# Four buffers in place of two for softmax numerators ahead of their DMA transposes

## The chip, the cores and the metric

One core of a Trainium2 chip. The metric is the device time of one execution in microseconds (us). Each run also records the mean clock granted to TensorE (1.0 is full). Engines in the profile: PE is TensorE, PEld its weight loads, DVE VectorE, ACT ScalarE, POOL GpSimd, SP SyncE; SPq is SyncE's queue of DMA issues. PSUM is, in this kernel, the memory that holds TensorE's scores and products.

## The reference, cut to what matters

```python
scores = (q @ k.T) / sqrt(64)                  # 8 batches x 8 heads, 576 x 576 each
scores = where(scores >= max(scores) - 0.02, scores, -1e9)
attn = exp(scores - max(scores)); attn /= attn.sum(-1)
x = (attn @ v) laid out as (8, 576, 512)
# then, per batch: h = relu(x @ w_in); u, v = halves of h; v normalized over features,
# mixed over positions by w_spatial plus a bias; out = (u * mixed v) @ w_out
```

The output is float32, 8 x 576 x 512.

## The kernel before

Two heads are a pair; there are 32 pairs. A pair's 512 first rows are four chunks of 128 (c = 0 to 3); the last 64 rows of two pairs share a chunk c = 4, worked in the odd pair. One chunk is one *step*, 144 in all; the steps of an odd pair come in the order 4, 0, 1, 2, 3. In a step TensorE makes the scores `s`, VectorE the maxima, ScalarE the exponentials. The numerators go to a buffer `p`, two chunks each, and one DMA transpose moves a full buffer to `pT`, which TensorE takes as weights for the product with v.

```python
p_ring = [const.tile([P, 2, 1152], BF16, name=f"p{i}") for i in range(2)]   # chunks 0,1 | 2,3
ptp = ctx.enter_context(tc.tile_pool(name="ptp", bufs=5))                    # pT
...
def mask():                                    # for the chunk of the step before
    i, c, e = unmasked.pop()
    ...
    pt = p_ring[c // 2]
    if not on_act(c):                          # chunks 0, 1, 3: VectorE writes p  (L541)
        nc.vector.scalar_tensor_tensor(out=pt[:, c % 2, :], in0=ef, scalar=ctau, in1=ef, ...)
    if c % 2:                                  # buffer full: transpose, from SyncE (L545)
        dst = pts[i, c // 2] = ptp.tile([P, 2, 9, P], BF16, name="pT")
        nc.sync.dma_start_transpose(out=..., in_=pt...)
...
def step(i, c, fs):
    s = scores(i, c)                           # TensorE (L519, L524)
    ...                                        # maxima on VectorE (L560)
    if on_act(c):                              # chunks 2 and 4
        for h in range(2): nc.scalar.activation(out=e[:, h, :], ..., func=ACT.Prelu, ...)  # L577
        nc.scalar.activation(out=pr_ring[i // 2 % 2] if c == 4 else p_ring[c // 2][:, c % 2],
                             in_=e..., func=ACT.Exp)                                       # L579
    else:
        for h in range(2): nc.scalar.activation(out=e[:, h, :], ..., func=ACT.Exp, ...)    # L583
    ...
    if unmasked: mask()
```

So chunk 2 is written by ScalarE in its own step, the others by VectorE one step late. The transpose of chunks 2 and 3 of an odd pair is issued in step 0 of the next pair, and ScalarE writes that buffer again in step 2.

## Time and profile before

| | before |
|---|---|
| timed runs, first call | 500.39, 500.67, 501.63, 503.14 us |
| profiled execution | 506.3 us (span 504.5), clock 0.973, state slow |
| TensorE, VectorE, ScalarE busy | 91%, 82%, 76% of the span |
| ScalarE idle before L579, for a transpose | 13.4 us in 6 places |
| VectorE idle before L541, for a transpose | 1.6 us in 1 place |

Busy shares say which engine is fullest. The idle time *before* an instruction, with what ended it, says which wait exists. Neither says alone what a wait costs. An engine *stands* while it is idle like this, and one such place is a *stop*. The lines are in the prediction below.

### The profile page before, as it was taken

The numbers are of one execution on the slowest core, as the hardware profiler recorded it, in microseconds if no ns is written. First come the engines' busy times: TensorE is split into PE (matmuls) and PEld (weight loads), VectorE is DVE, ScalarE is ACT, GpSimd is POOL, SyncE is SP. The second block draws the span as 40 slices with busy tenths as digits, with TensorE's granted clock in tenths as the row PEclk, the third lists the DMA queues.
The fourth block names the chain that finished last, engine by engine and source line by source line (L and its number), as shares of the span: only waits on it lengthen the run. The fifth ranks groups of instructions, "written<-read, shape, count | busy, mean of one in ns | idle before, by whom it ended". The sixth has DMA issues, their size and how long they took to land.

```text
span 504.5 us, 9916 instructions
## 1 busy us (share of the span) xinstructions
PE 459.3 (91%) x3672; PEld 244.8 (49%) x3672; DVE 412.4 (82%) x559; ACT 381.1 (76%) x665; POOL 224.5 (44%) x406
## 2 busy tenths in 40 slices
PE   7786977889988999979999999999999999997996
PEld 4342534445554545535455555545454545544543
DVE  2896696988989888868898888898889988897473
ACT  2784576798977888868887889787987889795251
POOL 3543312579535743246425753276425753251021
PEclk9997797999999999989999999999999999998999
DMA  7399789797999998987979998898987898667313
GB/s 229 64 222 244 176 174 180 197 212 162 203 193 205 169 210 170 186 158 160 224 178 194 181 201 191 192 196 170 220 201 176 179 214 181 136 119 116 116 63 126
DMA packets 231041, 89.38 MB, mean 177 GB/s; under 512 B 200593, under 2 KB 225169, under 8 KB 230993
## 3 DMA queue, kind: packets, MB, share of 16 engines
q1 hardware_dynamic: 230416, 87.93, 82.4%
q8 instruction: 29, 0.48, 0.4%
q0 software_dynamic: 160, 0.52, 0.3%
q10 hardware_dynamic: 416, 0.30, 0.2%
q14 instruction: 20, 0.16, 0.1%
HBM read 33.31 MB, written 9.44 MB: 85 GB/s over the span
## 4 chain that ended last, share of the span: by engine, by line
PE 51%; ACT 20%; DVE 12%; DMA 11%; issue 5%; POOL 0%; ACTq 0%; POOLq 0%; DVEq 0%
PE s L524 15%; DMA pT<-p 11%; ACT e L583 6%; DVE negm L560 6%; PE f L235 5%; PE s L519 5%; PE f L493 4%; DVE p L541 4%; PE f L268 3%; PE f L464 3%; ACT e L577 3%; PE f L434 3%; ACT vrel L402 2%; PE f L392 2%; ACT sq L416 2%
## 5 line engine op out<-in xcount | busy, mean ns | idle before, releaser
L560 DVE TENSOR_REDUCE negm<-s 128x2 f32<-128x1152 f32 x144 | 194.7, 1353 | 44.6 <-PE s L524 44.3
L524 PE MATMUL s<-qkT 64*128 64x512 f32 (+1 forms) x640 | 165.7, 651 | 0.0
L541 DVE SCALAR_TENSOR_TENSOR p<-e,ctau 128x1152 bf16<-128x1152 f32 x96 | 138.1, 1438 | 4.1 <-ACT e L583 2.2
L583 ACT ACTIVATE e<-s,negm 128x576 f32<-128x576 f32 x192 | 131.5, 739 | 6.3 <-DVE negm L560 6.2
L519 PE MATMUL s<-kd,qkT 128*128 128x128 f32 (+1 forms) x320 | 65.2, 308 | 18.0 <-ACT e L583 11.0
L577 ACT ACTIVATE e<-s,negm 128x576 f32<-128x576 f32 x96 | 65.7, 738 | 20.1 <-DVE negm L564 12.6
L258 POOL COPY kd<-qkT 64x64 f32<-64x64 f32 x64 | 27.8, 435 | 109.3 <-ACT qkT L253 107.3
L519 PEld LDWEIGHTS s<-kd,qkT 128*128 128x128 f32 (+1 forms) x320 | 45.8, 184 | 38.6 <-ACT e L583 21.6
L524 PEld LDWEIGHTS s<-qkT 64*128 64x128 f32 (+1 forms) x640 | 42.6, 177 | 18.6 <-issue 3.6
L268 PEld LDWEIGHTS <-pT 128*128 128x128 bf16 x1024 | 43.2, 99 | 10.8 <-issue 7.4
L579 ACT ACTIVATE p<-e 128x1152 bf16<-128x1152 f32 x32 | 37.2, 1164 | 14.3 <-DMA pT<-p 13.4
L410 POOL TENSOR_SCALAR nmean<-sm 128x1 f32<-128x1 f32 (+1 forms) x35 | 14.7, 420 | 73.3 <-ACT vrel L402 73.3
L268 PE MATMUL f<-v,pT 128*128 128x65 bf16 x992 | 46.3, 197 | 0.0
L138 POOL COPY qn<-ql 128x640 f32<-128x640 f32 x32 | 35.5, 1108 | 11.8 <-issue 6.5
L263 PE MATMUL f<-v,pT 128*128 128x130 bf16 x124 | 27.6, 223 | 11.0 <-ACT vrel L402 5.8
L464 PE MATMUL f<-wsT,vn 128*128 128x512 bf16 x120 | 30.9, 389 | 3.7 <-ACT qkT L253 3.7
L240 ACT ACTIVATE qkT<-f 128x512 f32<-128x512 f32 x32 | 18.9, 590 | 19.5 <-PE f L235 19.5
L242 ACT COPY qkT<-f 128x512 f32<-128x512 f32 x32 | 18.7, 586 | 17.3 <-PE f L235 17.2
L148 POOL CAST v<-vl 128x640 bf16<-128x640 f32 x32 | 30.1, 942 | 0.1
L422 POOL TENSOR_SCALAR vn<-vrel,rs,nm 128x512 bf16<-128x512 f32 (+1 forms) x34 | 27.4, 805 | 3.7
L392 PE MATMUL f<-w_in,xT 128*128 128x512 bf16 x112 | 28.9, 380 | 0.0
L434 PE MATMUL f<-xT,w_in 128*128 128x512 bf16 x108 | 27.9, 380 | 0.9 <-DVE xn L277 0.9
(155 smaller groups left out, 639.9 us busy)
## 6 DMA issues: line engine op xcount, KB each, us to landing
vl<-in_v_dram SPq DMA_DIRECT2D x16, 512.0 KB, 4.6
ql<-in_q_dram SPq DMA_DIRECT2D x15, 512.0 KB, 4.7
kl<-in_k_dram SPq DMA_DIRECT2D x15, 512.0 KB, 4.5
out_dram<-o SPq DMA_DIRECT2D x20, 256.0 KB, 3.1
uT<-in_moe_w_in_dram SPq DMA_DIRECT2D x3, 512.0 KB, 5.7
uT<-in_moe_w_spatial_dram SPq DMA_DIRECT2D x2, 576.0 KB, 5.8
vl<-in_v_dram SPq DMA_DIRECT2D x16, 64.0 KB, 4.3
pT<-p SPq DMA_TRANSPOSE x64, 5.0
```

The lines of the kernel that those rows point to most:

```text
L138: nc.gpsimd.tensor_copy(out=t, in_=ld_ring[i // 2 % 2][w][:, 2 * (i % 2):2 * (i % 2) + 2].rearrange("p h c d -> p c h d"))
L268: nc.tensor.matmul(out=t[:, at + 65 * h:at + 65 * h + 65], lhsT=pt[:, 5 * h + j, :], rhs=vt[:, 6 * h + j, :], start=False, stop=(h == 1 an ...
L392: nc.tensor.matmul(out=t, lhsT=xts[b][:, f, c * P:(c + 1) * P], rhs=w_in[:, f, 512:1024], start=(f == 0), stop=(f == 3))
L434: nc.tensor.matmul(out=t, lhsT=w_in[:, m, f * P:(f + 1) * P], rhs=xts[b][:, m, 0:512], start=(m == 0), stop=(m == 3))
L464: nc.tensor.matmul(out=t, lhsT=vn[:, c, f * P:(f + 1) * P], rhs=wsT[:, c, 0:512], start=(c == 0), stop=(c == 4))
L519: nc.tensor.matmul(out=view(s[rows], 512, [[448, 2], [1, 64]]), lhsT=qks[n][:, 0, m], rhs=kd_ring[n % 2], start=True, stop=True)
L524: nc.tensor.matmul(out=s[rows, 1024 * h:1024 * h + 512], lhsT=qks[n][hs, 0, m], rhs=qks[n][hs, 1, 0:512], start=True, stop=True)
L541: nc.vector.scalar_tensor_tensor(out=pt[:, c % 2, :], in0=ef, scalar=ctau, in1=ef, op0=ALU.is_ge, op1=ALU.mult)
L560: nc.vector.tensor_reduce(out=nm, in_=s, axis=AX.X, op=ALU.max, negate=True)
L577: nc.scalar.activation(out=e[:, h, :], in_=s[:, h, :], func=ACT.Prelu, bias=nm[:, h:h + 1], scale=by, alpha=1e30)
L579: nc.scalar.activation(out=pr_ring[i // 2 % 2] if c == 4 else p_ring[c // 2][:, c % 2], in_=e.rearrange("p h s -> p (h s)"), func=ACT.Exp)
L583: nc.scalar.activation(out=e[:, h, :], in_=s[:, h, :], func=ACT.Exp, bias=nm[:, h:h + 1])
```

## The change

The intent is that a write of numerators never waits for the transpose that still reads the buffer: each buffer comes again after two pairs (about 28 us) in place of one. Nothing else changes; the order of instructions on every engine is the same.

```diff
-    p_ring = [... for i in range(2)]
+    p_ring = [... for i in range(4)]
-        pt = p_ring[c // 2]
+        pt = p_ring[2 * (i % 2) + c // 2]
-            nc.scalar.activation(out=pr_ring[i // 2 % 2] if c == 4 else p_ring[c // 2][:, c % 2],
+            nc.scalar.activation(out=pr_ring[i // 2 % 2] if c == 4 else p_ring[2 * (i % 2) + c // 2][:, c % 2],
```

More of the change, by code (lines that the diff above doesn't have):

```diff
@@ L66 @@
     mhalf = const.tile([P, 1], F32, name="mhalf")
-    p_ring = [const.tile([P, 2, 1152], BF16, name=f"p{i}") for i in range(2)]
+    p_ring = [const.tile([P, 2, 1152], BF16, name=f"p{i}") for i in range(4)]
     pr_ring = [const.tile([P, 1152], BF16, name=f"pr{i}") for i in range(2)]
```

## The prediction

> **What bounds the kernel now.** I read the page first: its engine table, then the groups of instructions, then the chain that ended last.
>
> ```profile
> PE 459.3 (91%) x3672; PEld 244.8 (49%) x3672; DVE 412.4 (82%) x559; ACT 381.1 (76%) x665; POOL 224.5 (44%) x406
> ...
> PE 51%; ACT 20%; DVE 12%; DMA 11%; issue 5%; POOL 0%; ACTq 0%; POOLq 0%; DVEq 0%
> PE s L524 15%; DMA pT<-p 11%; ACT e L583 6%; DVE negm L560 6%; PE f L235 5%; PE s L519 5%; PE f L493 4%; DVE p L541 4%; PE f L268 3%; PE f L464 3%; ACT e L577 3%; PE f L434 3%; ACT vrel L402 2%; PE f L392 2%; ACT sq L416 2%
> ...
> pT<-p SPq DMA_TRANSPOSE x64, 5.0
> ```
>
> TensorE is the fullest engine, but the chain gives 11% of the span, 55 us, to the transposes of the numerators, the transfers whose source buffers the change doubles. That share is not what the change can win: the chain names a whole transfer as soon as it is the last releaser, even if the engine behind it stood for a moment. The view of the waits by releaser counts only standing time:
>
> ```profile
> ACT p L579 <- DMA pT<-p: 13.4, 6, 4.3
> ...
> PEld L263 <- DMA pT<-p: 9.6, 5, 3.3
> ```
>
> and the view of the tile p adds one VectorE wait of 1.6 us (L541). So at most 15.0 us of standing, in seven places, is the write-after-read wait on p. Six come before ScalarE's L579 (numerators of chunk 2, even pairs): by the timeline at 44.3 to 48.6 us (4.29), 75.1 to 78.2 (3.10), 158.8 to 160.7 (1.90), 216.6 to 219.8 (3.11), and 0.44 and 0.51 near 276 and 332 us. The other 26 writes by L579 wait for nothing. The even pairs suffer because chunk 2 of pair i+1 comes two steps after the transpose of chunks 2 and 3 of an odd pair i is issued, against three steps the other way round.
>
> Next question: what does TensorE do in those places? This is the timeline around the third.
>
> ```profile
> 159.76 1.09 PE L524 MATMUL s<-qkT 64*64 64x512 f32 x8
> ...
> 160.66 1.16 ACT L579 ACTIVATE p<-e 128x1152 bf16<-128x1152 f32 x1 [1.90 <-DMA pT<-p]
> 160.77 0.10 PEld L263 LDWEIGHTS <-pT 128*128 128x128 bf16 x1 [0.81 <-DMA pT<-p]
> ...
> 161.73 0.58 ACT L402 ACTIVATE vrel<-f 128x512 f32<-128x512 f32 x1
> ...
> 162.46 0.22 PE L263 MATMUL f<-v,pT 128*128 128x130 bf16 x1 [1.61 <-ACT vrel L402]
> ```
>
> TensorE has run ahead by two score blocks and then wants the product with pT of the previous odd pair: the result of the very transfer that ScalarE waits for. It landed at 160.58. From then TensorE is held only because its PSUM bank is to be freed by vrel (L402), which stands behind L579 in ScalarE's order. A part of each stop therefore stays after the change, as a read-after-write wait of TensorE, and only the part after the landing can go.
>
> **What the Trainium skill says.** (1) "TensorE: Matmul & The Clock Gate", Architectural detail under Part 1: "ACT/DVE are strict FIFO", and TensorE reorders weight loads only. The trace agrees: vrel at 161.73, whose product had ended by 158.84, waited behind L579. (2) Same page, Part 1, on the clock gate: the clock falls to half after about one idle window of 3413 ns, the window runs free, and a busy window restores it. The trace agrees in kind: the windows view shows granted clock 0.50 from about 44 to 57.6 us and 78 to 84.5 us, and 0.51 at 222 to 225 us, each after such a stop, and four score matmuls take 2.08 us there in place of 1.13. (3) "DMA: Bandwidth & Descriptors", Anatomy of one DMA: a semaphore wait happens on the issuing sequencer before dispatch. The trace agrees: the transpose issued at 40.44 us stands behind four loads of 0.5 to 0.6 us each on SyncE and lands 8.0 us after its issue. The buffer count of p changes nothing in that queue.
>
> ```profile
> 42.00:45.00 3.00, 0.78 (x12) 0.35 (x8) 2.97 (x4) 1.37 (x2) 0.17 (x1) 0.84 1.17 208
> 45.00:48.00 3.00, 1.93 (x10) 0.25 (x8) 1.90 (x4) 0.00 (x0) 1.72 (x3) 0.50 1.08 244
> ...
> 57.00:60.00 3.00, 3.00 (x28) 1.36 (x26) 2.04 (x5) 1.33 (x4) 1.43 (x4) 0.89 1.02 249
> ```
>
> (Columns: window, length, then busy time of TensorE, weight loads, VectorE, ScalarE and GpSimd, granted clock, DMA share, GB/s. ScalarE is at 0.00 in the second line: that is the stop.)
>
> **The change part by part.** *Added and removed instructions*: none. The order of instructions on all five engines is the same in both kernels; only buffer names and a few waits differ. Three waits of the writers of p go because they are first uses, one each appears on the writers of pr and of two outputs, and four on xr; all of these name transfers of buffers last used about a pair of pairs earlier (some 28 us), so I count them as zero. *Memory*: two more buffers of 2x1152 bf16, 4.6 KB a partition each; it builds. *Moved*: a write of p now waits for a transpose two pairs back, some 28 us, against landings of 4.6 to 8.4 us. All seven waits should go: 15.0 us of standing to zero.
>
> *What that is worth on the path*, by stop, as TensorE's idle time after the landing:
> - 48 us: after pT lands the product runs 48.5 to 49.8; the next scores wait 1.23 us for e (L583), which stood behind L579. Gain 1.23.
> - 78 us: the same picture, 1.23.
> - 160 us: TensorE is free at 160.85, starts at 162.46. Gain 1.61.
> - 219 us: landing 219.69, start 221.54 behind vrel. Gain 1.83.
> - 276 and 332 us: 0.16 and 0.22.
> Sum 6.3 us. VectorE's 1.6 us at 39.9 counts nothing extra: TensorE would only reach the 48.5 us landing earlier and stand longer.
>
> *Clock*: at 219 us the idle falls from 3.27 to about 1.4 us, like the 1.61 us at 160 us that lost no clock. The work after 221.54 ran at half clock (L464 x5 2.32 us in place of 1.24, products 1.1 in place of 0.6); without that, about 1.6 us less. At 48 and 78 us the long idle stays, but TensorE then works without the second gap, and may get its clock back one window earlier; one window at half speed is 1.7 us of lost work each, and I give that four chances in ten: 1.4. Ceiling by this trace 6.3 + 1.6 + 1.4 = 9.3 us.
>
> *Cut*: this profiled run took 506.3 us, 4.7 over the median of the timed runs, so some of these stops, most likely that at 219 us with its clock loss (3.4 us), are smaller or absent there. Without it: 9.3 - 3.4 = 5.9. Not all will be kept, as VectorE is nearly full in the first 100 us (2.9 to 3.0 of 3 us in most windows outside the stops) and the DMA engines are 83 to 95% busy; I keep eight tenths: 4.8 us. Predicted 501.63 - 4.8 = 496.8 us, 1% less.
>
> **The rivals.**
> *A: the wait only changes hands.* The products need the same transposes two steps later, and DMA or SyncE sets the pace; TensorE's waits for pT grow by what ScalarE's shrink. For it: DMA at 0.95 in 104 to 160 us, the shared landing in the timeline, transposes held in SyncE's order. Against it: in four of six stops TensorE demonstrably stands 1.2 to 1.8 us after the landing, and later stretches without stops have TensorE at 54.5 of 56 us. Then 500 to 501.6 us.
> *B: the loops tighten more than the sum says.* ScalarE comes earlier to the numerators of chunk 3's partner, so the next transpose is issued earlier, later stops shrink too, and the two cold stretches (about 13.6 and 6.5 us at half clock) vanish altogether, worth up to 10 us. For it: the cold stretch at 44 us begins just when TensorE stands 2.23 us behind ScalarE and VectorE's delayed work. Against it: pT lands at 48.5 whatever p does, so TensorE is idle some 4 us there anyway. Then 489 to 492 us.
> *C: slower.* Earlier transposes collide with loads. Against it: the traffic and its order are the same, and SyncE issues strictly in order. At most 1 or 2 us.
>
> **Range and chances.** A and the sum bound the likely region: 492.5 to 500.8 us. A gain over 2% means under 491.6 us, that is B nearly whole: 0.07. Slower by 2% (over 511.7) has no mechanism here: 0.01. Within 2%: 0.92.
>
> **What would show it.** Right: no wait of L579 or L541 for pT<-p; the transposes' share of the chain gone from ScalarE and coming back, smaller, through L263; TensorE's waits for pT the same or larger in sum (now 12.7 us); vrel no longer releasing L263 for over 1 us; steady batches still 55.5 to 56 us. Wrong, towards A: the waits at L263 grow by 10 us or more and the span stays. Wrong, towards B: granted clock near 1.0 through 44 to 85 us. The prediction fails too if the unprofiled runs have stops in other places than this one trace.

## The result, and the profile after

| | before | after |
|---|---|---|
| median of the first call | 501.15 us (4 runs) | 488.84 us (4 runs: 488.69, 488.74, 488.93, 496.58) |
| ratio of the fast runs | | 0.9747, 95% interval 0.9711 to 0.9784 |

Ratios here are the mean time of one kernel's fast runs over that of the other's of the same rounds, so not quite the ratio of the medians quoted. A run counts as slow when it is over 1.5% above its kernel's fastest.

From the page of the kernel after: the engines, the chain that ended last, and the group of L579, whose last column (idle before it) names no transpose any more.

```profile
PE 451.2 (93%) x3672; PEld 240.6 (49%) x3672; DVE 413.4 (85%) x559; ACT 382.0 (78%) x665; POOL 228.7 (47%) x406
...
PE 46%; DVE 23%; ACT 18%; issue 6%; DMA 4%; SPq 2%; POOL 0%; DVEq 0%; ACTq 0%
...
L579 ACT ACTIVATE p<-e 128x1152 bf16<-128x1152 f32 x32 | 37.2, 1164 | 1.0
```

The view of the waits of the kernel after has neither L579 nor L541 waiting for pT<-p. What is left of the waits for transposes is TensorE's:

```profile
PEld L263 <- DMA pT<-p: 5.6, 4, 2.3
...
PE f L263 <- DMA pT<-p: 2.2, 2, 1.4
```

Before, these were 9.6 and 3.1 us. So TensorE's waits for the same transposes did not grow in exchange; in this profile they shrank. Over all profiles they neither shrank nor grew clearly: 12.7, 7.2 and 6.4 us before, 7.8, 8.2, 10.7 and 8.0 us after (one stop can count under both PEld and PE). This is the timeline at the place that the prediction showed (chunk 2 of pair 10, then the product of pair 9):

```profile
149.81 1.17 ACT L579 ACTIVATE p<-e 128x1152 bf16<-128x1152 f32 x1
...
150.78 1.09 PE L524 MATMUL s<-qkT 64*64 64x512 f32 x8
...
150.88 0.58 ACT L402 ACTIVATE vrel<-f 128x512 f32<-128x512 f32 x1
...
151.79 0.10 PEld L263 LDWEIGHTS <-pT 128*128 128x128 bf16 x1 [0.81 <-DMA pT<-p]
151.80 0.23 PE L263 MATMUL f<-v,pT 128*128 128x130 bf16 x1
```

L579 waits for nothing, vrel (L402) follows it 1.07 us later, the bank is free, and the product starts as soon as TensorE has ended its scores. TensorE wants pT 2.0 us after ScalarE wanted the buffer (151.80 against 149.81); in those 2.0 us the transpose lands.

A place-by-place comparison: I took the start of the chunk 2 write of each pair from the timelines (L579; L540 in the kernel that moves it). "To pair 5" is the first six pairs with the start of the kernel; "5 to 31" the other 26. The last column adds up the idle time before that write for a transpose, within 5 to 31.

| profile | to pair 5, us | 5 to 31, us | 13 to 31, us | ScalarE standing in 5 to 31, us |
|---|---|---|---|---|
| before, first (slow) | 93.3 | 365.7 | 255.9 | 5.96 |
| before (ctrl_before, slow) | 88.4 | 366.7 | 257.2 | 6.74 |
| before (before_second, slow) | 91.3 | 361.7 | 252.6 | 3.27 |
| two buffers with fillers (warm_before, fast) | 90.4 | 362.9 | 254.1 | 3.94 |
| after, first (fast) | 83.8 | 359.3 | 250.8 | 0 |
| after_again, after_third, after_fourth (fast) | 86.5, 85.3, 85.7 | 359.6, 358.9, 358.6 | 250.8, 250.8, 250.8 | 0 |

From pair 13 on the kernel after takes 250.8 us in every profile. The kernel before takes 1.8 to 6.4 us more, and over 5 to 31 its excess over the mean of the four (359.1) is 6.6, 7.6 and 2.6 us for 5.96, 6.74 and 3.27 us of standing. The three profiles of the kernel before fell on runs that count as slow (499.9 to 506.3 us), so the difference must also show in a fast one. It does: warm_before, described below, took 500.3 us and counts as fast, its additions all come before chunk 2 of pair 5, and its 5 to 31 is 3.8 us over for 3.94 us of standing. The first six pairs wander in both.

### The profile page after: what moved, and what is told of

It reads as the page before. It is cut to its first block, busy times and chain, and to the rows that moved or that the text cites. A ratio compares the mean times of both kernels' runs of the same rounds, so it can differ in the third digit from the quotient of the medians.

```text
span 486.9 us, 9920 instructions
## 1 busy us (share of the span) xinstructions
PE 451.2 (93%) x3672; PEld 240.6 (49%) x3672; DVE 413.4 (85%) x559; ACT 382.0 (78%) x665; POOL 228.7 (47%) x406
## 4 chain that ended last, share of the span: by engine, by line
PE 46%; DVE 23%; ACT 18%; issue 6%; DMA 4%; SPq 2%; POOL 0%; DVEq 0%; ACTq 0%
PE s L524 13%; DVE negm L560 11%; DVE p L541 8%; PE f L235 5%; PE f L493 4%; ACT e L583 4%; PE s L519 4%; ACT e L577 4%; PE f L268 3%; DMA pT<-p 3%; PE f L434 3%; PE f L464 3%; ACT sq L416 2%; ACT vrel L402 2%; ACT qkT L242 1%
## 5 line engine op out<-in xcount | busy, mean ns | idle before, releaser
L524 PE MATMUL s<-qkT 64*128 64x512 f32 (+1 forms) x640 | 163.8, 642 | 0.0
L541 DVE SCALAR_TENSOR_TENSOR p<-e,ctau 128x1152 bf16<-128x1152 f32 x96 | 140.2, 1461 | 1.5 <-ACT e L583 1.2
L268 PEld LDWEIGHTS <-pT 128*128 128x128 bf16 x1024 | 41.9, 98 | 7.2 <-issue 3.9
L268 PE MATMUL f<-v,pT 128*128 128x65 bf16 x992 | 44.9, 194 | 0.0
L579 ACT ACTIVATE p<-e 128x1152 bf16<-128x1152 f32 x32 | 37.2, 1164 | 1.0
L464 PE MATMUL f<-wsT,vn 128*128 128x512 bf16 x120 | 29.8, 378 | 3.7 <-ACT qkT L253 3.7
L277 DVE TENSOR_TENSOR xn<-f,r 128x256 bf16<-128x256 f32 x62 | 26.3, 425 | 2.1
L422 POOL TENSOR_SCALAR vn<-vrel,rs,nm 128x512 bf16<-128x512 f32 (+1 forms) x34 | 26.3, 772 | 3.7
```

The source lines that it names most:

```text
L268: nc.tensor.matmul(out=t[:, at + 65 * h:at + 65 * h + 65], lhsT=pt[:, 5 * h + j, :], rhs=vt[:, 6 * h + j, :], start=False, stop=(h == 1 an ...
L464: nc.tensor.matmul(out=t, lhsT=vn[:, c, f * P:(f + 1) * P], rhs=wsT[:, c, 0:512], start=(c == 0), stop=(c == 4))
L524: nc.tensor.matmul(out=s[rows, 1024 * h:1024 * h + 512], lhsT=qks[n][hs, 0, m], rhs=qks[n][hs, 1, 0:512], start=True, stop=True)
```

## The experiments

My theory after the result: the gain is ScalarE's standing before L579, as everything behind it in ScalarE's order stands too, plus what the loss of TensorE's clock after such a stop adds. Rivals: VectorE's one wait starts the first stop; the clock alone is the gain; the first result was luck.

| run | what differs from the kernel before | mean us (runs) | before in the same call | ratio of fast runs, 95% |
|---|---|---|---|---|
| ctrl_before | nothing | 499.5 (22) | 499.2 (59) | 0.997 (0.994 to 1.001) |
| p1_only | chunks 2, 3 doubled | 492.0 (6) | 499.2 (59) | 0.984 (0.979 to 0.988) |
| p0_only | chunks 0, 1 doubled | 500.6 (22) | 499.2 (59) | 1.004 (1.001 to 1.007) |
| warm_before | filler matmuls | 500.4 (22) | 499.2 (59) | 1.002 (0.999 to 1.004) |
| after_again | the change | 492.8 (6) | 499.8 (27) | 0.986 (0.982 to 0.990) |
| ring3 | three buffers in turn | 492.3 (6) | 499.8 (27) | 0.985 (0.981 to 0.990) |
| late_exp | two buffers, write one step later | 494.1 (4) | 499.8 (27) | 0.989 (0.983 to 0.995) |
| pool_loads_after | the change, loads from GpSimd | 507.9 (21) | 499.8 (27) | 0.992 (4 fast runs of 21) |
| after_third | the change | 493.3 (16) | 498.8 (43) | 0.990 (0.987 to 0.993) |
| warm_after | the change, filler matmuls | 492.0 (6) | 498.8 (43) | 0.989 (0.982 to 0.995) |
| w_late_after | the change, later loads of w_in | 493.3 (15) | 498.8 (43) | 0.993 (0.990 to 0.996) |
| late_exp_b | as late_exp | 494.5 (19) | 498.8 (43) | 0.994 (0.991 to 0.997) |
| after_fourth | the change | 492.8 (6) | 499.3 (27) | 0.988 (0.982 to 0.993) |
| before_second | nothing | 499.3 (20) | 499.3 (27) | 0.997 (0.994 to 1.001) |

All results were correct. The means are over all runs, slow ones too; with one core the kernel before scatters over some 15 us, and the rule for "fast" drops a tenth to a half of its runs in a call and none of the changed kernel's later ones, so the ratios understate the gain a little (after_third: 0.990, against 0.989 of the means of all runs). I give both. pool_loads_after is the reverse case: its ratio rests on its four best runs.

**ctrl_before.** No edit.

> The kernel before, unchanged, as a control. Every theory: ratio 1.00, fast runs at 500 to 503 us. It is to show how far equal kernels scatter, and, in its profile, whether the half-clock stretches after about 44 us and 78 us and at about 220 us are there in a run that is not of the slow state. Theory 1 (the clock that TensorE loses after the stops is half of the gain) expects the first two in every profile; theory 2 (the first profile was an unlucky one and the stops themselves are the gain) expects at most one of the three.

Equal within the interval, but its 22 runs went from 494.1 to 505.1 us, and the kernel before's own 59 in that call from 492.4 to 506.8. The three runs that I had predicted from (500.4 to 503.1) were neither its level nor its spread. Of the three half-clock stretches that I had named, only a shorter one at 48 to 54 us was there, as theory 2 allowed; others were near 21, 63 and 330 us. The stops are in the later batches again, at the same even pairs, but with other sizes. The timeline of its largest, before chunk 2 of pair 22:

```profile
325.35 1.09 PE L524 MATMUL s<-qkT 64*64 64x512 f32 x8
...
326.97 0.10 PEld L263 LDWEIGHTS <-pT 128*128 128x128 bf16 x1 [1.41 <-DMA pT<-p]
327.01 1.16 ACT L579 ACTIVATE p<-e 128x1152 bf16<-128x1152 f32 x1 [2.65 <-DMA pT<-p]
...
328.08 0.58 ACT L402 ACTIVATE vrel<-f 128x512 f32<-128x512 f32 x1
...
328.80 0.22 PE L263 MATMUL f<-v,pT 128*128 128x130 bf16 x1 [2.36 <-ACT vrel L402]
```

The transpose frees the buffer and brings pT at the same moment, 326.97; TensorE, free at 326.44, starts at 328.80, held by vrel. From the chunk 2 write of pair 21 to that of pair 22 took 15.73 us, against 13.11 in the kernel after: 2.62, the whole standing of 2.65. The next interval took 16.64 in place of 15.38, under half clock:

```profile
327.00:330.00 3.00, 1.15 (x20) 0.98 (x22) 1.40 (x4) 2.99 (x7) 0.57 (x3) 0.98 1.14 235
330.00:333.00 3.00, 3.00 (x9) 1.27 (x7) 1.94 (x3) 2.97 (x5) 2.81 (x5) 0.50 0.66 140
```

(Windows view, columns as in the prediction: the clock, third from the end, falls to 0.50.)

**p1_only and p0_only.** Three buffers each.

```diff
-        pt = p_ring[c // 2]
+        pt = p_ring[c // 2 * (1 + i % 2)]             # p1_only, in L579 too
+        pt = p_ring[1 if c > 1 else 2 * (i % 2)]      # p0_only, in L579 too
```

> Only the buffer of chunks 2 and 3 is doubled (three buffers). Theory 1: the wait of ScalarE before L579 is what holds everything behind it, so this gives nearly all of the gain: ratio 0.975 to 0.98, 489 to 491 us. Rival (the wait of VectorE on the buffer of chunks 0 and 1 near 40 us starts the first stop and with it the loss of clock): at most half of the gain, ratio 0.985 to 0.99.

> Only the buffer of chunks 0 and 1 is doubled (three buffers). Theory 1: VectorE's single wait of 1.6 us goes, the six of ScalarE stay: ratio 0.995 to 1.0. Rival (that wait starts the first stop): ratio 0.985 to 0.99, and no half-clock stretch from 44 us.

p1_only: 492.0 us, 7.2 under the kernel before. Its ratio, 0.984, lies between what the two theories expected; both took the first call's gain as the size to share out. But its 5 to 31 is 359.3 us as with four buffers, its 13 to 31 250.7. VectorE still waits 2.2 us once for the other buffer. p0_only: no gain; ScalarE keeps seven waits (from the view of its waits):

```profile
ACT p L579 <- DMA pT<-p: 12.5, 7, 4.1
```

So the buffer of chunks 2 and 3 carries the gain, and the rival "VectorE's wait starts it" falls.

**warm_before and warm_after.** Nine matmuls without a use, in the places where TensorE idled in the first profile, with two and with four buffers. (The fillers also take one more PSUM tile in two steps.)

```diff
+            if part == 1:
+                keep_warm(t, i + 2, {1: 2, 3: 3}.get(i, 0))   # before the product of pairs 1, 3
...
+        if c == 4 and i in (3, 5):
+            keep_warm(bank(), i, {3: 3, 5: 1}[i])             # before the scores of chunk 4
```

> Two buffers as before; nine score-like matmuls of about 0.57 us without a use stand where TensorE idles at 42 to 48 us (three before the scores of chunk 4 of pair 3, two before the product of pair 1) and at 75 to 78 us (one and three, of pairs 5 and 3). All waits on p stay. Theory 1: TensorE keeps its clock there, the half-clock work of about 3.6 and 2.5 us goes, ratio 0.986 to 0.992 (494 to 497 us). Rival (the gain is the standing behind ScalarE alone): ratio 0.998 to 1.003.

The mean clock rose from 0.982 to 0.989, and the time did not fall. I then guessed that the fillers cost some 3 us and hid a gain:

> Four buffers with the same nine filler matmuls that did not help the kernel before. If the fillers cost time where TensorE isn't idle (theory 1: some 3 us, which hid a gain of about 2 us by the clock in the kernel before), then here, with less clock left to win, the time is 2 to 4 us over the four-buffer kernel in this call, at a clock of 0.99 or more. Rival (fillers are free, and the clock in the first 90 us is worth nothing): equal within 1 us.

That missed: with four buffers they brought no loss (492.0 against 493.3 us), at a clock of 0.997. So more clock, by this means, bought nothing with two buffers, and my clock terms for the first 90 us have no support. It isn't shown that they are zero: a cost of the fillers that just equals what the clock gives would look the same. (Some runs of the kernel before do show faster times at higher clocks, but a long stop both takes time and lowers the clock, so that alone proves nothing.)

**after_again, after_third, after_fourth.** The changed kernel again, on three chips.

> The changed kernel unchanged, once more, beside many runs of the kernel before (which scattered from 492 to 507 us on the last chip). Theory 1 (the change takes two things: the stops in the later batches, 6 to 7 us in every run, and 2 to 8 us of the first 90 us, where chance rules): ratio 0.975 to 0.983, and runs that scatter less than those of before, mostly 488 to 492 us; the last 26 pairs in the profile take 359.3 us as in the first profile of it. Rival (the first measurement was luck): ratio 0.985 or above, like the run with one buffer doubled.

> The changed kernel a third time, for the size of the gain. Pooled so far: before 499.4 us mean of 103 runs at a mean granted clock of 0.981, after 492.0 of 10 runs at 0.987. Theory 1 (a steady 6 to 7 us from the stops of the later batches, and the rest is chance of the clock): ratio 0.982 to 0.990, mean 490 to 494 us. Rival (the first result, 0.9747, is the true size and the second one was unlucky): ratio 0.971 to 0.979.

> The changed kernel on whatever chip this call gets. If the first result is the chip's[...], some chips give a tight group under 489 us and others 490.4 to 496; if it was chance, the runs lie at 490 to 496 us here too and the ratio at 0.984 to 0.991.

28 runs together: mean 493.1 us, from 490.4 to 496.1, all fast. The kernel before in these calls and those of the controls: 198 runs, mean 499.3, from 491.6 to 508.5. The gain is 6.2 us, 1.2%; against the 126 fast ones among the 198 (mean 497.6) it is 4.5 us, 0.9%. The first call's 12.3 us did not come again: after_again fell where its rival put it, and after_fourth nearly where chance put it (490.7 to 496.1 us, 0.988). Three of the first call's four runs of the changed kernel lie under all 28 later ones, which chance alone hardly gives; the chip of that call is not known to me, so whether it was the chip stays open.

**ring3.** Three buffers in turn.

```diff
-        pt = p_ring[c // 2]
+        pt = p_ring[(2 * i + c // 2) % 3]             # in L579 too
```

> Three buffers taken in turn, so a buffer comes again after one and a half pairs, some 21 us. If only the wait on a landed transpose matters (landings take at most 8.4 us), both theories expect it equal to four buffers: ratio within 0.5% of that of after_again in this call, no wait of L579 or L541 for pT<-p. If doubling chunk 0 and 1's buffer as well is what separates the four-buffer kernel from the run with one buffer doubled, this shows it too.

492.3 us against 492.8 with four, no wait of ScalarE or VectorE for a transpose, 5 to 31 in 358.7 us. One and a half pairs are enough, with 4.6 KB a partition less.

**late_exp and late_exp_b.** Two buffers; chunk 2's write goes behind ScalarE's work on chunk 3.

```diff
-            nc.scalar.activation(out=pr_ring[...] if c == 4 else p_ring[c // 2][:, c % 2], ...)
+            if c == 4:
+                nc.scalar.activation(out=pr_ring[...], ...)
...
 def mask():
+        if c == 2:
+            nc.scalar.activation(out=pt[:, 0], in_=e..., func=ACT.Exp)
```

> Two buffers; the numerators of chunk 2 are written one step later, after the scores' part of chunk 3 on ScalarE, so ScalarE does other work while the transpose lands. Theory 1 (what costs is that ScalarE's queue stands behind L579 in its order): the stops of up to 3.1 us in the later batches go, the last 26 pairs take 359 to 361 us in place of 365 to 367, ratio 0.982 to 0.99. Rival (what costs is the landing itself, through the write of p or through the product): the time stays, ratio 0.997 to 1.003.

> The two-buffer kernel with the late write of chunk 2's numerators again, for its size (494.05 us of 4 runs). Theory 1 (the standing of ScalarE in the later batches is the steady gain, however it is removed): within 2 us of the four-buffer kernel of this call, last 26 pairs within 1.5 us of 359.5 us. Rival (more buffers give something besides): 3 us or more over it.

This is the run that separates "the landing is late" from "ScalarE stands at it". The transposes land no sooner (median 5.4 us from issue, 5.0 in the first profile of before), yet ScalarE's waits in 5 to 31 are gone, because it does other work first. The timeline of late_exp at chunk 2 of pair 10 (in this kernel's lines L586 is the exponential of chunk 3, L540 the moved write, and L579 the first step of the next chunk):

```profile
150.79 1.37 ACT L586 ACTIVATE e<-s,negm 128x576 f32<-128x576 f32 x2 [0.25 <-DVE negm L562]
152.05 1.16 ACT L540 ACTIVATE p<-e 128x1152 bf16<-128x1152 f32 x1
153.10 1.37 ACT L579 ACTIVATE e<-s,negm 128x576 f32<-128x576 f32 x2
```

The two profiles take 251.1 and 251.3 us from pair 13 to 31, within 0.5 us of four buffers. Over 5 to 31 they take 362.3 and 360.7, so the first missed the 359 to 361 expected, in pairs 5 to 13; the second keeps one stop of 1.35 us before pair 5. With 494.4 us as the mean of the 23 runs of both calls it gives 4.9 of the 6.2 us (3.2 of 4.5 against fast runs alone), for no memory.

**pool_loads_after.** Four buffers, the later loads of q, k and v issued from GpSimd.

```diff
-                    queue.extend(load(i + (3 if g else 2), 2, w))
+                    queue.extend(load(i + (3 if g else 2), 2, w, nc.gpsimd))
...
-            nc.sync.dma_start(                        # rest_b, the last rows of v
+            eng.dma_start(
```

> Four buffers, and the loads of q, k and v after the first pairs issued from GpSimd in place of SyncE, so that no transpose stands behind them in SyncE's order. Theory 1 (the transposes of odd pairs are late because they stand behind four loads of 0.6 us): TensorE's waits for pT in the first 90 us shrink from 7.8 us to under 4, ratio to before 0.968 to 0.977. Rival (the transposes are late because the DMA engines are full): waits for pT stay at 6 us or more, ratio as after_again or worse[...].

Much worse, 490.9 to 528.2 us, against 490.4 to 493.9 of after_again in the same call. The idea was that transposes stand behind loads in SyncE's order, so taking those away should bring them sooner. In the one profile, of a run of 526.2 us, they landed later: a median of 6.4 us from issue in place of 5.2 in after_again, and up to 19.1 in place of 8.1. TensorE's waits for pT in the first 90 us were 21.0 us in place of 6.6. (The 7.8 us of the expectation was the whole first profile of after; its first 90 us had 6.2.) From the page of this run, the share of the DMA engines by queue, and from its waits:

```profile
q1 hardware_dynamic: 192256, 60.89, 67.1%
q0 software_dynamic: 8560, 27.56, 21.4%
...
PE f L263 <- DMA pT<-p: 22.7, 9, 4.7
```

The Trainium skill, "DMA: Bandwidth & Descriptors", Issuing engines are not separate DMA queues, says that DMAs from any engine run on the same 16 DMA engines and interleave, and that another issuer saves only issue time. The run agrees and adds that here it costs. That SyncE's order had also kept loads and transposes apart is my guess; how the DMA engines share themselves between the two queues, no run here shows.

**w_late_after.** Four buffers, the w_in loads at steps 14, 16, 18 and 20 (their casts at 17 to 23).

> Four buffers, and the four loads of w_in (512 KB each) some 5 steps later, at steps 14, 16, 18 and 20 in place of 8, 11, 14 and 17, out of the transfers around the transpose of pair 1. If TensorE's remaining waits for pT in the first 90 us (7.8 us in the first profile of the four-buffer kernel) come of these loads beside the transposes, they fall to 4 us or less and the time by 2 to 4 us under the four-buffer kernel of this call; if they only move to the next odd pairs, it is equal within 1.5 us.

493.3 us, as after_third in the same call, and TensorE's waits for pT were 11.9 us in its profile against 10.7 (11.1 against 9.9 in the first 90 us, where the expectation's 7.8 should read 6.2). The lateness in the first 90 us is not these four loads' alone.

**before_second.** No edit, for one more profile.

> The kernel before with one more profile. Theory (the gain lies in the later batches alone): in a usual run, 497 to 500 us, the first six pairs take 86 to 89 us, near the 84 to 86.5 us of the four-buffer profiles, and the last 26 pairs 364 to 367 us against 359.5. Rival (half of the gain is in the first 90 us): 90 us or more there in a usual run.

Its profiled run (499.9 us) took 91.3 us to pair 5 and 361.7 for the rest: both expectations missed in part, as there was more in the first six pairs and less in the later ones than either said. It began with the same two half-clock stretches (near 12 and from 21 us) as after_again, which took 86.5 us to pair 5.

## Why the prediction was wrong, point by point

- **Which waits go: right.** All waits of L579 and L541 went, and none came in their place.
- **Rival A, the wait changes hands: wrong in the later batches.** TensorE wants the same transpose about 2.0 us after ScalarE; in the three profiles of before, only two of the 14 standings in pairs 5 to 31 were longer than that (3.11 and 2.65 us).
- **Rival B, the loops tighten: not borne out.** Its sign came in the first profile of after (clock 1.00 from 30 to 102 us), and its 489 to 492 us all but met the first call. In the later profiles the sign came in after_again only, and their runs' mean of 493.1 us lies outside, so I call that nearness luck.
- **The later stops, 5.4 us with the clock at 219 us: right in kind, a little small.** The same trace was 6.6 us over the four-buffer kernel in 5 to 31. The excess over three profiles follows ScalarE's whole standing, not only TensorE's idle time after the landing.
- **The step that failed: "Cut".** I struck out 3.4 us, as the stop at 219 us would be "smaller or absent" in runs without a profile. It does shrink (0.52 us in before_second, 1.57 in ctrl_before), but every profile of before has stops at pairs 10, 14, 18 and 22; one grows where another shrinks, and their sum was 3.3 to 6.7 us. Reading one trace's stop as an accident, I struck out a part of the steady cost. After "Cut" and "eight tenths" the sum held 1.6 us for the later batches; the profiles give 5.6 in the means, and 2.6 in before_second, nearest to a usual run.
- **"I keep eight tenths": wrong there as well.** Pairs 13 to 31 take 250.8 us in each profile without these waits. Nothing is given back there. The two cuts took 4.6 us; without them the sum is 9.3, which is 3.0 under the first call's gain and 3.1 over that of all later runs. So they explain a part of the miss, and the rest stays open.
- **The first 90 us, 3.9 us with the clock: mis-sized.** The profiles of before took 88.4 to 93.3 us to pair 5, those of after 83.8 to 86.5, 5.7 us in the means, where the sum held 3.1 after "eight tenths". My step "at 48 and 78 us the long idle stays" failed in the first profile of after: TensorE idled 0.78 and 1.42 us at these landings in place of 1.59 and 1.55, and the clock stayed at 1.00. In after_third it did stay (3.5 us, then half clock), so it varies by run. The windows of the first profile of after, as shown of before:

```profile
42.00:45.00 3.00, 2.32 (x25) 1.27 (x24) 2.97 (x4) 1.64 (x4) 1.25 (x1) 1.00 1.34 260
45.00:48.00 3.00, 1.46 (x12) 0.41 (x12) 2.97 (x5) 2.97 (x5) 1.89 (x3) 1.00 0.93 197
```

- **Slips in the working.** The clock at 44 us did not fall "after such a stop": it was at half from 44.0 us, after a wait of TensorE for ScalarE, and L579 began to stand at 44.3. Eight tenths of 5.9 is 4.7, not 4.8. The 1.7 us per window is an estimate, half of the window that the prediction cites; no run here shows it. What shows that SyncE waits before it issues is its own idle time (67.4 us in 46 places before L545, for VectorE's numerators), not the four loads named.
- **The range: built on too few runs.** I took 501.63 us from three runs as the level and gave no room for the scatter of either kernel, 17 us and 8 us from end to end. The time of the first call, 488.84, fell out of the range by 3.7 us. Of the 28 later runs the mean is within it.
- **What stays open.** The profiles give 5.7 + 5.6 us for the two stretches and 0.4 after them, the timed runs 6.2 in all. The profiled runs of before were slow ones (502.8 us in the mean of three, 499.3 over all runs) and those of after quick ones (491.1 against 493.1), 5.5 us between them, so the sum of the profiles is too high; how a usual run shares 6.2 us between the first 90 us and the later batches, and why the first call gave twice as much, is not settled. Its profiled run was 3.2 us quicker than the three later ones: 2.1 us up to pair 5 and 1.5 us after the last chunk 2 write, none of it in the stops' stretch.

## What to carry to other kernels

When an in-order engine waits for a buffer that a DMA is still reading, count its whole standing if another engine needs that DMA's result only later: what stands behind the write is what costs. One buffer more does as much as doubling all, and moving the write behind other work of the same engine does most of it (4.9 of 6.2 us here). Before striking out a stop as an accident of one trace, profile the kernel twice, and take the level from tens of runs when a handful already spread by half a per cent.

## What the Trainium skill lacked or had wrong

- "TensorE: Matmul & The Clock Gate", summary table: it asks for no idle gaps over about 3 us. In the first profile of after the clock fell to 0.50 at 22.0 us with no gap over 1.25 us just before, so a gap well under 3 us is not safe by itself (elsewhere the page does tell of short idles that did this). Nor does the busy time alone decide: TensorE was busy 1.75 of 3 us from 18 us and 1.87 from 21 us there, and just as much in the first profile of before, where the clock stayed at 1.00.
- Same page, Part 1: it puts the penalty of the ramp under 1% of a typical span. It says that the ramp varies by run, but not how far the times of equal runs may scatter: 491.6 to 508.5 us here, at clocks of 0.922 to 0.996. The runs do not show how much of it the clock causes: warm_before had 0.006 more clock and no less time.
- "DMA: Bandwidth & Descriptors", on issuing engines: it gives no figure for what moving loads to GpSimd may cost the transposes issued from SyncE (here, in one profile of a slow run, the median landing went from 5.2 to 6.4 us, the longest from 8.1 to 19.1).
- "DMA: Bandwidth & Descriptors", Latency and other measured facts: it gives 261 GB/s as the effective bandwidth of a DMA transpose with a non-contiguous middle dimension, which makes 2.3 us for the 590 KB here (an estimate), and no time beside other transfers. In the profiles of both kernels a transpose of 128x2304 bf16 landed 4.6 to 8.5 us after its issue.
